# Four first products before the first second product, and a PSUM bank moved from transposes to first products

## The chip, the cores and the metric

The kernel runs on one core of a Trainium2 chip. The metric is device time in microseconds (us) of one execution. The kernel before takes 1392.38 us, the median of 3 runs (1392.05, 1392.38 and 1400.18 us).

## The reference

Three layers follow each other. An attention with queries averaged in pairs gives 2304 tokens of 512 numbers. A mixture of 8 experts sends each token to the one expert with the largest gate logit. A third layer works on all tokens with a cosine gate. All arrays that come in are 32-bit here except that the last layer's weights are narrowed by the kernel from 64-bit words.

```
xe = x[mask]                       # the tokens of expert e
h  = np.maximum(xe @ w1[e], 0.0)   # 512 -> 1024, the "first product"
ye = h @ w2[e]                     # 1024 -> 512, the "second product"
out[mask] = gate_w[mask, None] * ye
...
h = x @ w_in
g = h * np.cos(h)
return g @ w_out
```

## The kernel before

**Stages.** The attention of 4 batches by 8 heads comes first, with the routing of each batch's tokens after it. Then come the experts, in 12 units: a unit is up to 256 tokens of one expert. The units per expert are (3, 2, 2, 1, 1, 1, 1, 1), so units 0 to 2 belong to the busiest expert, and units 10 and 11 hold 128 tokens at most. The cosine layer in 5 blocks of up to 512 tokens ends the kernel.

**A unit.** Its tokens are gathered from memory and transposed on the PE into a PSUM tile of the pool `px` (tag `pt`), which ACT copies out as `xh` (line 1069) and DVE as the remainder `xl` (line 1070). The hidden width of 1024 is cut in four chunks. For a chunk, `first` (lines 903 to 926) makes 24 matmuls into one bank of the pool `ph`; ACT then writes `hh` with a relu (line 924), and DVE the remainder `hl` (line 925), so the bank is free when both are done. `second` (lines 951 to 966) makes 12 matmuls from `hh` and `hl` into the two banks of `py`. A chunk's `first` and `second` are called F0 to F3 and S0 to S3 below. The pending list holds `ahead` chunks, HP in number, before the oldest one's `second` is written; with HP = 2 the order is F0 F1 F2 S0 F3 S1 S2 S3. A unit's results go out with ACT (line 985) and DVE (line 986) and a DMA on ACT's queue (line 987). In units of 128 tokens (`tokens_first`, `turned`) the pending length is 0 whatever HP is, but their products and transposes also take `ph` tiles.

**Work between.** After S0, S1, S2 and S3 the function `second` writes the work of `between[c]`: in an expert's last unit the load of chunk c of the weights of the expert two further on, and two steps of `Narrow` in units 2 to 8. A load is two DMAs on SP's queue into three raw buffers, two casts on ACT (line 1057) and two subtractions on DVE or POOL (line 1058). A chunk's w2 cast overwrites the weights which the S of that chunk reads, two experts alternating between two sets. A step narrows a tile of 64-bit words: a DMA on SP's queue, four instructions on DVE (lines 1110, 1113, 1116, 1119), two on ACT (1115, 1118), two on POOL (1120, 1121), and a store on ACT's queue (1130), with four buffers of each kind. Steps are placed behind the latest relu on ACT's queue by `issue_after(self.relu)`.

**Order.** The program's order is a priority: a planner simulates the engines at build time and fixes each engine's queue, so instructions of different parts interleave (the transposes of a unit's tokens stand at the end of the unit before). On the chip each engine runs its queue in that order and waits at the head. The eight PSUM banks of this stage take the place of those of the attention, whose pools `at_ps2` (3), `at_psm` (3, also used by the routing) and `at_ps1` (2) are opened in this order.

Of the kernel before, what the change touches and what calls it, by code (L numbers as in the profile page):

```python
# [16 lines left out]
PSUM = bass.MemoryType.PSUM  # L17
# [27 lines left out]
class Attention:  # L45
# [15 lines left out]
    def __init__(self, tc, ctx, pools, q, k, v, ident, xpool):  # L61
        nc = self.nc = tc.nc
        self.tc = tc
        self.q, self.k, self.v = q, k, v
        self.ident = ident
        self.xpool = xpool

        cp, self.pw, self.pk, self.p3, ce, self.p1 = (pools[k] for k in "cwksep")
        self.ps2 = ctx.enter_context(tc.tile_pool(name="at_ps2", bufs=3, space=PSUM))
        self.psm = ctx.enter_context(tc.tile_pool(name="at_psm", bufs=3, space=PSUM))  # L70
        self.ps1 = ctx.enter_context(tc.tile_pool(name="at_ps1", bufs=2, space=PSUM))
        self.idr = cp.tile([P, P], F32R, name="idr")
        nc.vector.tensor_copy(self.idr, ident)
        self.k2, self.q1, self.q2, self.va, self.mm, self.qr, self.pe = [], [], [], [], [], [], []

        def const(kept, pools, name, shape, dt=F32):
            kept += [p.tile([P] + shape, dt, name=f"{name}_{i}") for i, p in enumerate(pools)]

        self.mx = []
        const(self.qr, (cp,) * 2, "qr", [5, 2 * D])  # L80
        const(self.mm, (cp,) * 2, "mm", [5, 3])
        const(self.pe, (cp,) * 2, "pe", [5, 66])
        const(self.mx, (cp,) * 4, "mx", [5], F32R)
        const(self.q1, (ce, ce, ce, cp), "q1", [SQ + 64], F32R)
        const(self.k2, (ce, cp, ce), "k2", [S], F32R)
        const(self.q2, (ce, ce, ce, cp), "q2", [SQ], F32R)
        const(self.va, (cp, cp, ce, ce, ce), "va", [NK, 130], F16)
        self.st = {}
        self.xf, self.xs = {}, {}
# [380 lines left out]
ZAT = 2  # L470
ZU = 11
MPOOL = ((), (0, 1, 2, 3))
HP = 2
NSTEP = (0, 2, 8, 8, 8, 8, 8, 8, 8, 6, 0, 0)

LOAD1 = ((1, 2), (1, 3), (2, 0), (2, 1))
# [406 lines left out]
class Experts:  # L883
    def __init__(self, tc, ctx, w1, w2, y_d, rp, ident, ahead):
        self.ahead = ahead
        self.tc, self.nc = tc, tc.nc
        self.w1, self.w2, self.y_d = w1, w2, y_d
        self.rp, self.ident = rp, ident
        self.p2 = ctx.enter_context(tc.tile_pool(name="ex_p2", bufs=2, reuse_waits="tile"))
        self.ph = ctx.enter_context(tc.tile_pool(name="ex_ph", bufs=3, space=PSUM, reuse_waits="tile"))  # L890
        self.px = ctx.enter_context(tc.tile_pool(name="ex_px", bufs=3, space=PSUM, reuse_waits="tile"))
        self.py = ctx.enter_context(tc.tile_pool(name="ex_py", bufs=2, space=PSUM, reuse_waits="tile"))

    def chunk(self, name, e, c, to):
# [312 lines left out]
def body(ctx, tc, q, k, v, w_gate, w1, w2, w_in, w_out, out):  # L1207
# [104 lines left out]
    with mid as s:  # L1312
        ns = ExitStack()
        nw = ns.enter_context(tc.tile_pool(name="nw", bufs=4, side="right", reuse_waits="tile"))
        ex = Experts(tc, s, w1, w2, y_d, rp, ident, HP)
        narrow = Narrow(nc, nw, jobs)
# [119 lines left out]
```

## Time and profile before

| | |
|---|---|
| median of 3 runs | 1392.38 us |
| the profiled execution's own time | 1388.87 us |
| its span on the core | 1387.3 us |
| mean granted clock of the PE | 0.955 |
| PE busy | 1246.8 us (90%) |
| DVE busy | 1081.0 us (78%) |
| ACT busy | 737.7 us (53%) |
| POOL busy | 674.3 us (49%) |

The busy times are sums over the whole span; the stages differ in what limits them, so the sections below read them by stretch. The profiled execution is 3.5 us under the median of the runs.

### The profile page before, as it was taken

The numbers are of one execution on the slowest core, as the hardware profiler recorded it, in microseconds if no ns is written. First come the engines' busy times: TensorE is split into PE (matmuls) and PEld (weight loads), VectorE is DVE, ScalarE is ACT, GpSimd is POOL, SyncE is SP. The second block draws the span as 40 slices with busy tenths as digits, with TensorE's granted clock in tenths as the row PEclk, the third lists the DMA queues.
The fourth block names the chain that finished last, engine by engine and source line by source line (L and its number), as shares of the span: only waits on it lengthen the run. The fifth ranks groups of instructions, "written<-read, shape, count | busy, mean of one in ns | idle before, by whom it ended". The sixth has DMA issues, their size and how long they took to land. (4 is left out here: it accounts for less than half of the span.)

```text
span 1387.3 us, 27417 instructions
## 1 busy us (share of the span) xinstructions
PE 1246.8 (90%) x10190; PEld 1051.3 (76%) x10190; DVE 1081.0 (78%) x2075; ACT 737.7 (53%) x1695; POOL 674.3 (49%) x623
## 2 busy tenths in 40 slices
PE   5897997999979998999799887889899999999996
PEld 4686886887768887878777776777687888888885
DVE  6996988888879998864598789896965666667674
ACT  4685875777758875872364455555322323222232
POOL 6684876666568777641367667675302002001010
PEclk9898999999989998999999898999999999999998
DMA  8348345333543342415687667787102001000000
GB/s 178 93 115 184 87 104 70 87 79 83 126 70 87 79 108 58 113 32 102 184 262 227 208 212 261 244 269 228 45 0 64 1 0 61 1 11 35 1 31 16
DMA packets 126911, 146.24 MB, mean 105 GB/s; under 512 B 35888, under 2 KB 83120, under 8 KB 126768
## 3 DMA queue, kind: packets, MB, share of 16 engines
q1 hardware_dynamic: 108784, 114.97, 32.7%
q0 software_dynamic: 5600, 15.25, 3.6%
q10 hardware_dynamic: 12384, 14.17, 3.4%
q8 instruction: 82, 1.34, 0.4%
q14 instruction: 61, 0.50, 0.1%
HBM read 97.57 MB, written 28.43 MB: 91 GB/s over the span
## 5 line engine op out<-in xcount | busy, mean ns | idle before, releaser
L319 POOL TENSOR_TENSOR pl<-pf,ph 128x576 f16<-128x576 f32 x220 | 310.5, 1420 | 138.3 <-ACT ph L309 59.3
L297 ACT ACTIVATE pf<-pst 128x288 f32<-128x288 f32 x576 | 222.0, 419 | 101.2 <-PE pst L289 84.2
L263 DVE TENSOR_REDUCE mm<-pm 128x1 f32<-128x384 f32 x432 | 226.7, 546 | 45.0 <-PE pm L254 37.5
L288 PE MATMUL pst<-q,k 128*128 128x288 f32 x576 | 195.6, 346 | 0.1
L289 PE MATMUL pst<-q,k 66*128 66x288 f32 x576 | 172.3, 308 | 24.5 <-DMA q<-mx 24.5
L484 POOL DMA_INDIRECT out_dram<-os,token x18 | 18.2, 1012 | 347.8 <-ACT os L1200 182.5
L338 PE MATMUL po<-va,pl 128*128 128x66 f16 (+1 forms) x1440 | 178.0, 197 | 1.9 <-DVE pl L319 1.0
L336 PE MATMUL po<-va,ph 128*128 128x66 f16 (+1 forms) x1440 | 179.4, 197 | 0.3 <-ACT pe L342 0.3
L337 PE MATMUL po<-va,ph 128*128 128x64 f16 (+1 forms) x1440 | 177.2, 196 | 0.0
L254 PE MATMUL pm<-k,q 128*128 128x384 f32 x384 | 151.2, 412 | 19.1 <-DVE mm L263 15.8
L1171 ACT ACTIVATE a<-a,hpi 128x512 f32<-128x512 f32 (+1 forms) x80 | 54.5, 681 | 210.8 <-DVE a L1170 210.8
L336 PEld LDWEIGHTS <-ph 128*128 128x128 f16 (+1 forms) x1440 | 136.4, 102 | 25.4 <-issue 11.2
L338 PEld LDWEIGHTS <-pl 128*128 128x128 f16 (+1 forms) x1440 | 137.8, 102 | 14.9 <-issue 5.6
L337 PEld LDWEIGHTS <-ph 128*128 128x128 f16 (+1 forms) x1440 | 138.0, 102 | 7.7 <-issue 2.5
L289 PEld LDWEIGHTS pst<-q,k 66*128 66x128 f32 x576 | 113.4, 198 | 26.5 <-DMA q<-mx 17.5
L309 ACT CAST ph<-pf 128x576 f16<-128x576 f32 x191 | 129.5, 681 | 1.4 <-PE po L337 0.4
L1161 PE MATMUL ch<-zh,w1h_m 128*128 128x512 f32 (+1 forms) x320 | 118.9, 372 | 4.5 <-ACTq L1385 3.4
L1161 PE MATMUL ch<-zl,w1h_m 128*128 128x512 f32 (+1 forms) x320 | 118.7, 371 | 0.0
L1161 PE MATMUL ch<-zh,w1l_m 128*128 128x512 f32 (+1 forms) x320 | 118.5, 370 | 0.0
L288 PEld LDWEIGHTS pst<-q,k 128*128 128x128 f32 x576 | 113.0, 197 | 4.9 <-ACT pf L297 1.3
L1185 PE MATMUL po<-w2h_m,gh 128*128 128x512 f32 x288 | 114.1, 396 | 0.0
L1185 PE MATMUL po<-w2l_m,gh 128*128 128x512 f32 x288 | 113.8, 395 | 0.0
(262 smaller groups left out, 3386.5 us busy)
## 6 DMA issues: line engine op xcount, KB each, us to landing
w1r_e<-in_moe_w_dram SPq DMA_DIRECT2D x32, 512.0 KB, 5.2
w2r_e<-in_moe_w_dram SPq DMA_DIRECT2D x32, 512.0 KB, 5.4
kr<-in_k_dram SPq DMA_DIRECT2D x32, 288.0 KB, 3.2
vr<-in_v_dram SPq DMA_DIRECT2D x32, 288.0 KB, 3.0
k<-k SPq DMA_DIRECT2D x32, 288.0 KB, 4.4
q<-q SPq DMA_DIRECT2D x60, 144.0 KB, 2.4
qr<-in_q_dram SPq DMA_DIRECT2D x32, 256.0 KB, 3.5
raw<-in_moe_w_in_dram SPq DMA_DIRECT2D x32, 256.0 KB, 4.2
```

The source lines that it names most:

```text
L254: nc.tensor.matmul(ps[:, :384], self.st[i]["q1"][:, q0 : q0 + P], self.st[i]["k1"][:, ks], start=True, stop=True)
L263: self.nc.vector.tensor_reduce(self.mm[i % 2][:, ci, g : g + 1], self.st[i]["pm", ci, g][:, :384], axis=AX.X, op=ALU.max)
L288: nc.tensor.matmul(ps[:, :288], s["k1"][:, ks], s["q1"][:, o], start=True, stop=False)
L289: nc.tensor.matmul(ps[:, :288], self.k2[i % 3][: D + 2, ks], self.q2[i % 4][: D + 2, o], start=False, stop=True)
L297: nc.scalar.activation(s["pf", c][:, j * 288 : (j + 1) * 288], s["pst", c, j][:, :288], AF.Exp, scale=0.0625)
L309: nc.scalar.copy(ph, pf)
L319: low = eng.tensor_sub(s["pl"][:, c, :], s["pf", c], s["ph"][:, c, :])
L336: nc.tensor.matmul(po[:, :66], hi, va[:, c, D:130], start=(c == 0), stop=False)
L337: nc.tensor.matmul(po[:, :D], hi, va[:, c, :D], start=False, stop=False)
L338: self.product = nc.tensor.matmul(po[:, :66], lo, va[:, c, D:130], start=False, stop=(c == NK - 1))
L1161: nc.tensor.matmul(ph[:, :n], wt[:, c, fs], z[:, c, :n], start=(k == 0), stop=(k == 3 * NDC - 1))
L1185: nc.tensor.matmul(po[j], g[:, ts], wt[:, f % FC, :], start=(f == 0 and k == 0), stop=(f == NFC2 - 1 and k == 2))
```

## The change

HP goes from 2 to 3, so that a unit's order becomes F0 F1 F2 F3 S0 S1 S2 S3, and the `hh` and `hl` tiles get four buffers in place of three. The pool `ph` gets four PSUM banks in place of three, and `px` two in place of three.

```diff
-HP = 2
+HP = 3
...
-        self.ph = ctx.enter_context(tc.tile_pool(name="ex_ph", bufs=3, space=PSUM, reuse_waits="tile"))
-        self.px = ctx.enter_context(tc.tile_pool(name="ex_px", bufs=3, space=PSUM, reuse_waits="tile"))
+        self.ph = ctx.enter_context(tc.tile_pool(name="ex_ph", bufs=4, space=PSUM, reuse_waits="tile"))
+        self.px = ctx.enter_context(tc.tile_pool(name="ex_px", bufs=2, space=PSUM, reuse_waits="tile"))
```

## Rows read from the trace of the kernel before

**Rows 1.** Busy time by stretch: PE, PEld, DVE, ACT, POOL; clock, DMA share, GB/s.
```profile
708.00:920.00 212.00, 179.22 (x1062) 155.75 (x1061) 186.81 (x318) 111.58 (x207) 148.24 (x140) 0.91 0.76 239
...
955.00:1387.30 432.30, 410.30 (x1883) 335.65 (x1881) 290.00 (x495) 125.67 (x202) 55.03 (x54) 0.99 0.09 29
```

**Rows 2.** The PE's timeline in units 3 to 9, its waits and one F3.
```profile
718.90 0.50 PE L957 MATMUL py_u<-w2h_e,hh_u 128*128 128x512 f32 x1 [2.03 <-ACT hh_u L924]
720.78 0.80 PE L957 MATMUL py_u<-w2h_e,hl_u 128*128 128x512 f32 x1 [1.14 <-DVE hl_u L925]
...
760.54 0.79 PE L957 MATMUL py_u<-w2h_e,hh_u 128*128 128x512 f32 x1 [2.24 <-ACT hh_u L924]
...
777.64 0.79 PE L957 MATMUL py_u<-w2h_e,hh_u 128*128 128x512 f32 x1 [3.07 <-ACT hh_u L924]
...
781.46 0.80 PE L957 MATMUL py_u<-w2h_e,hl_u 128*128 128x512 f32 x1 [2.60 <-DVE hl_u L925]
...
785.21 0.29 PE L918 MATMUL ph_u<-xh_e,w1h_e 128*128 128x256 f32 x1
...
788.06 0.39 PE L957 MATMUL py_u<-w2h_e,hh_u 128*128 128x512 f32 x1
...
807.60 0.50 PE L957 MATMUL py_u<-w2h_e,hh_u 128*128 128x512 f32 x1 [1.49 <-ACT hh_u L924]
810.60 0.50 PE L957 MATMUL py_u<-w2h_e,hl_u 128*128 128x512 f32 x1 [2.26 <-DVE hl_u L925]
...
839.22 0.79 PE L957 MATMUL py_u<-w2h_e,hh_u 128*128 128x512 f32 x1 [3.12 <-ACT hh_u L924]
846.25 0.80 PE L957 MATMUL py_u<-w2h_e,hl_u 128*128 128x512 f32 x1 [5.82 <-DVE ys_u L986]
...
874.08 0.33 PE L1067 MATMUL pt_e<-ident,xg_e 128*128 128x128 f32 x1 [2.13 <-DMA xg_e<-x_d,ix_e]
...
879.07 1.22 PE L957 MATMUL py_u<-w2h_e,hl_u 128*128 128x512 f32 x2 [4.67 <-DVE hl_u L925]
...
905.43 0.50 PE L957 MATMUL py_u<-w2h_e,hl_u 128*128 128x512 f32 x1 [1.73 <-DVE hl_u L925]
```

**Rows 3.** Busy time by stretch: units 4, 5 and 7, each from F0 to F0.
```profile
738.30:765.80 27.50, 25.26 (x156) 22.32 (x154) 21.81 (x43) 15.32 (x31) 18.65 (x19) 0.94 0.75 232
765.80:797.30 31.50, 25.83 (x155) 22.33 (x153) 25.78 (x48) 13.18 (x27) 19.63 (x21) 0.89 0.64 203
...
827.30:862.10 34.80, 25.86 (x156) 22.43 (x154) 33.86 (x55) 19.48 (x34) 27.05 (x23) 0.85 0.77 255
```

**Rows 4.** Busy time by stretch: S0 of unit 4, and S0 of unit 5.
```profile
746.90:749.70 2.80, 2.80 (x14) 2.29 (x13) 2.80 (x1) 1.56 (x4) 2.36 (x4) 1.00 0.48 171
777.60:785.20 7.60, 4.96 (x12) 3.52 (x13) 4.82 (x7) 2.27 (x5) 3.81 (x4) 0.55 0.70 245
```

**Rows 5.** DVE's waits, 687 to 920 us: total us, times, longest.
```profile
DVE v L1110 <- DMA wo_d<-v: 8.6, 5, 2.8
DVE w1l_e L1058 <- ACT w1h_e L1057: 4.6, 3, 2.4
...
DVE xl_e L1070 <- ACT xh_e L1069: 1.4, 1, 1.4
```

**Rows 6.** ACT's waits in the same stretch.
```profile
ACT w1h_e L1057 <- DMA w1r_e<-in_moe_w_dram: 27.8, 12, 6.2
...
ACT w2h_e L1057 <- PE py_u L957: 12.1, 2, 7.3
```

**Rows 7.** PE's timeline: F3 of unit 0, tokens of unit 2, unit 10.
```profile
637.27 0.28 PE L918 MATMUL ph_u<-xh_u,w1h_e 128*128 128x256 f32 x1
...
674.87 0.87 PE L1067 MATMUL pt_e<-ident,xg_e 128*128 128x128 f32 x4 [4.69 <-DMA xg_e<-x_d,ix_e]
...
926.60 0.44 PE L946 MATMUL phT_u<-ident,hs_u 128*128 128x128 f32 x2 [3.38 <-ACT hs_u L940]
```

**Rows 8.** DVE's timeline: it reads the last PSUM tile of the routing.
```profile
645.63 0.20 DVE L692 TENSOR_TENSOR ro<-pr,bo 128x40 f32<-128x40 f32 x1 [3.07 <-PE pr L682]
```

## The prediction

> **What bounds the kernel now.** I read the busy times by stretch first, since the change touches the expert stage alone. From 708 to 920 us, units 3 to 9, PE is busy for 179.2 of 212 us and DVE for 186.8, its densest stretch with all other queues working too; from 955 us to the end PE is busy for 410.3 of 432.3 us [rows 1]. So a microsecond that the expert stage hands over early is kept by the PE-bound cosine layer, and the question is what sets the pace in the 212 us.
>
> PE's timeline shows where it stands still: at the start of S0, waiting for `hh` of chunk 0 and then for `hl` of it [rows 2]. The waits are 2.03 + 1.14 = 3.17 us in unit 3, none in unit 4 (there S3 waits for 2.24), 3.07 + 2.60 = 5.67 in unit 5, 3.75 in unit 6, 8.94 in unit 7, 2.13 + 4.67 = 6.80 in unit 8 and 1.73 in unit 9, 32.3 us in all with unit 4's. F3 stands behind S0 in PE's queue. With three `ph` banks it could not have been started there anyway: its bank is chunk 0's, which the same late `hl` frees. PE is therefore held by a reader on another engine and by a missing bank together, which is what the change takes up.
>
> Then the side that makes `hl` late. DVE's and ACT's own waits name memory and each other more than PE: DVE waits 8.6 us for the buffer of a narrowing store, ACT 27.8 us for w1 to arrive, and for PE only 12.1 us, twice [rows 5, 6]. In unit 7, 34.8 us long, DVE is busy for 33.86 us [rows 3]: no reordering on PE makes that unit's side work shorter by more than a microsecond.
>
> **Part 1, F3 ahead of S0.** F3 takes 788.06 - 785.21 = 2.85 us [rows 2]. Put into the wait it hides min(2.85, wait): 2.85 in units 3, 5, 6, 7 and 8, 1.73 in unit 9, 15.98 us. The relu of chunk 3 now stands ahead of the load and steps of `between[0]` on ACT, so unit 4's 2.24 for `hh` at S3 should go as well: 18.2 us, the upper end, if `hl` of chunk 0 stays as late behind F0 as it is. The lower end is one 2.85: if DVE and ACT keep their absolute times, F3 gains its place once, and after that PE merely arrives 2.85 earlier at each S0 and waits 2.85 longer.
>
> Between these ends I look at what two neighbouring units did. S0 of unit 4 found its operands ready, and the unit took 27.5 us; unit 5 then waited for 5.67 and took 31.5, together 59.0 [rows 2, 3]. Time that PE won was largely given back one unit later, so I start from the lower end. What the side can speed up by is DVE's waiting for ACT, 4.6 + 1.4 = 6.0 us [rows 5], since ACT's relus no longer sit behind a weight cast that waits for S0. Of that I take half, 3.0; its ends are 0 and 6.0. Sum for units 3 to 9: 2.85 + 3.0 = 5.85.
>
> What is late next is `hl` of chunks 1 and 2, which S1 and S2 now want with no F3 between; S1 starts 2.80 us after S0, the length of an undisturbed S0 [rows 4]. That is part of why I don't take the upper end.
>
> **The wait also costs clock.** S0 of unit 5 has PE 4.96 us busy at a granted 0.55, near the lower of its two levels (1.2 and 2.4 GHz), against 2.80 at 1.00 in unit 4 [rows 4]. 2.16 us would come back there if the wait fell away; but 5.67 - 2.85 = 2.82 us of it stays, so I count none.
>
> **Part 2, what else moves.** Chunk 0's load and its two steps now follow the relu of chunk 3. On SP's and POOL's queues their order against other DMAs and gathers does not depend on a relu. On ACT they come later by at most F3's 2.85, hidden as long as S0 itself waits, since the w2 cast must wait for S0 in either order. Without that cover the cost is the slow rival below.
>
> Units 0 and 1 lie ahead of the stretch: PE waits 4.69 us there for the gathered tokens of unit 2 [rows 7], which come from the routing, so what PE wins before is waited for again. Zero. The fourth `ph` bank is one of the routing's: its last tile is read at 645.63 [rows 8], while unit 0's F3 starts at 637.27 [rows 7]. Bound: 8.4 us later, of which 4.69 are covered, so 0 to 3.7; I take 0, as the bank may be any of three and the planner can put S0 first.
>
> Two `px` banks hold the two transposed tiles of one unit, and the next unit's come over 25 us later [rows 3]. Zero, by that cover; without it a transpose would wait for DVE as S0 does now, 1.73 to 8.94 us. In units 10 and 11 PE waits 3.38 us for `hs` [rows 7]; a fourth `ph` bank lets a further product fill it: 0 to 3.4, I take 1.5.
>
> **Sum.** 5.85 + 1.5 = 7.35 us. Against the profiled execution (span 1387.3, itself 1388.87) that gives 1381.5; that execution is 3.5 us under the median of 1392.38. The median after is predicted at 1392.4 - 7.4 = 1385.0, with 1379 to 1391 as this case's own range (gains of 13 to 1).
>
> **Two rules that pull opposite ways.** The gaps ahead of S0 recur in six of seven units, with lengths from 1.73 to 8.94 [rows 2]. The Trainium skill ("Perfetto Trace Analysis", Optimization Strategy) says that a gap that repeats on the engine which should be saturated can mean there is not enough PSUM for the next tile. By it the fourth bank gives the upper end, 18.2 us; that the lengths differ fivefold speaks for a backlog instead. The same page (Identifying the Most-Contended Engine) judges Vector by occupancy and Tensor by the share of weight loads, and works on the highest first. Here that is DVE, 186.8 against 155.75 of 212 us [rows 1], and by it PE's order gives next to nothing.
>
> **Rivals.**
> - *Full gain, 0.21.* The side follows PE: relus and casts come earlier as S1 to S3 close up, each unit keeps its F3. 1392.4 - 18.2 = 1374. For it: DVE has 25 us without work in the 212 [rows 1], enough for 18. Against it: 8.6 of DVE's waits are for stores [rows 5].
> - *The side alone sets the pace, 0.23.* Only one F3 is won, or the planner goes on placing S0 ahead of F3 where it thinks `hl` is ready, and the change does not do what it says. 1389 to 1393. For it: unit 7 in rows 3, and the pair of units 4 and 5.
> - *Slower, 0.11.* Place: ACT's cast of w2 chunk 0, which waits for the end of S0. From the point where `hl` of chunk 0 is ready before F3 ends, S0 ends 2.85 later than now, and ACT's queue (steps, stores, the next relus) stands behind that cast. Units 4, 6, 7, 8 and 9 load weights: 5 x 2.85 = 14.3, so 1407. For it: this wait is 12.1 us already [rows 6]. Against it: only unit 4 has `hl` in time now.
> - The forecast has the remaining 0.45.
>
> **Range and chances.** About 1% (13.9 us) is what a measurement of this kernel can tell from no change. The range 1372 to 1396 holds the forecast, the full gain and the one-off, with the start's bound above it, and leaves out the slow case and some tails. Faster by over 1% (below 1378.5): nearly all of the full gain and a tail of the forecast, 0.21. Slower by over 1%: most of the slow case, 0.09. Within: 0.70.
>
> **What would show it.** In the trace after, PE's S matmuls of a unit should follow each other with F3 ahead of all. Right: waits at S0 shorter by under 3 us in unit 3, but not in the later units, whose S0 start a few us earlier in absolute time; DVE over 90% busy from 708 us. Full gain: those waits shorter by 2.85 each and the cosine layer starting some 18 us before 955. Slow: ACT's waits for `py_u` well above 12.1 us, and no wait of PE for `hl`. The prediction is wrong if the planner shuffles the steps and loads so that DVE's queue has another order altogether, which no row here can tell.

## The result: 1.3% slower

The changed kernel takes 1411.9 us, the median of four runs (1409.6 to 1416.33), against 1392.85 us for the kernel before in the same comparison (1392.05 to 1400.18). The ratio is 1.013, with a 95% interval of 1.0103 to 1.0157. That is 19 us more, outside the range of 1372 to 1396, and on the other side of the forecast. The profiled execution after takes 1411.51 us, its span is 1409.9 us and the mean granted clock 0.947.

The first reading is by stage. I cut both traces at PE's own marks: the attention's last product, the first product of unit 2, of unit 10 and of the cosine layer. These are the stretches before (columns: stretch in us and its length, then busy us and instruction count of PE, PEld (its weight loads), DVE, ACT and POOL; granted clock, DMA share, GB/s):

```profile
623.90:684.30 60.40, 53.30 (x329) 45.80 (x325) 31.88 (x114) 18.47 (x30) 15.54 (x16) 0.94 0.61 128
684.30:919.70 235.40, 202.62 (x1215) 176.85 (x1213) 203.84 (x345) 126.13 (x232) 159.50 (x150) 0.92 0.76 240
919.70:955.30 35.60, 30.14 (x178) 26.07 (x177) 28.68 (x39) 21.93 (x39) 20.41 (x18) 0.90 0.75 241
```

And the same stretches after, with units 3 to 9 alone as the third row and the cosine layer as the last:

```profile
628.50:699.10 70.60, 55.87 (x333) 48.21 (x332) 34.33 (x116) 18.95 (x30) 15.95 (x16) 0.82 0.48 118
699.10:928.70 229.60, 200.63 (x1212) 175.32 (x1210) 181.62 (x320) 121.78 (x225) 159.59 (x143) 0.92 0.75 233
722.50:928.70 206.20, 177.23 (x1059) 154.19 (x1057) 170.08 (x296) 108.01 (x200) 150.88 (x136) 0.91 0.76 236
928.70:979.70 51.00, 30.53 (x179) 26.04 (x176) 32.44 (x60) 30.16 (x52) 33.38 (x30) 0.84 0.84 267
979.70:1409.90 430.20, 411.78 (x1880) 337.38 (x1880) 283.75 (x495) 121.51 (x197) 46.81 (x49) 0.98 0.07 23
```

The spans differ by 22.6 us. The attention ended 4.6 us later (628.5 against 623.9), which is no effect of the change: up to there PE, DVE, ACT and POOL run the same instructions in the same order, and the attention's end lies between 622.0 and 635.1 us over all the traces of this study. The start of the experts costs 10.2 (60.4 to 70.6). Units 2 to 9 gain 5.8 (235.4 to 229.6), and units 10 and 11 lose 15.4 (35.6 to 51.0). The cosine layer is 1.8 shorter (1387.3 - 955.3 = 432.0, and 430.2). So in this trace the middle of the stage, which the prediction worked out most closely, came near what it said (the experiments below show that the nearness is within the scatter), and two edges that it had priced at nothing, or as a small gain, decided the time.

**The start.** PE's timeline after, just behind the attention (start, duration, instruction; in brackets the idle time before it and what ended it):

```profile
642.17 0.19 PE L675 MATMUL pr<-oh,tri 128*128 128x40 f16 x1 [6.20 <-DVE oh L654]
642.20 0.26 PE L677 MATMUL pr<-oh,ones 128*128 128x32 f16 x4
642.31 0.28 PE L682 MATMUL pr<-oh,ones 128*128 128x8 f16 x5
642.44 0.56 PE L918 MATMUL ph_u<-xh_u,w1h_e 128*128 128x256 f32 x1
...
672.26 1.09 PE L1067 MATMUL pt_e<-ident,xg_e 128*128 128x128 f32 x4 [5.30 <-DMA xg_e<-x_d,ix_e]
```

The first product of unit 0 stands directly behind the last products of the routing, at 642.44, that is 13.9 us after the attention's end. Before, it came 0.1 us after that end, and F3 of unit 0 started at 637.27 while the routing still ran [rows 7]. PE's wait for the tokens of unit 2 is still there, 5.30 us against 4.69 [rows 7]. The 10.2 us of this stretch are 7.6 more without work on PE (70.60 - 55.87 = 14.7 against 60.40 - 53.30 = 7.1) and 2.6 more busy, at a granted clock of 0.82 in place of 0.94. The 13.9 us ahead of F0 are not all lost, as PE makes the routing's products in them, which before ran between those of unit 0.

**Units 3 to 9.** The same view, the waits ahead of second products that answer to those of before [rows 2], of a microsecond or more:

```profile
759.98 0.50 PE L957 MATMUL py_u<-w2h_e,hh_u 128*128 128x512 f32 x1 [1.27 <-ACT hh_u L924]
765.15 0.80 PE L957 MATMUL py_u<-w2h_e,hl_u 128*128 128x512 f32 x1 [4.43 <-DVE hl_u L925]
...
794.45 0.79 PE L957 MATMUL py_u<-w2h_e,hl_u 128*128 128x512 f32 x1 [3.42 <-DVE hl_u L925]
...
852.84 0.79 PE L957 MATMUL py_u<-w2h_e,hh_u 128*128 128x512 f32 x1 [7.22 <-ACT hh_u L924]
859.71 0.80 PE L957 MATMUL py_u<-w2h_e,hl_u 128*128 128x512 f32 x1 [5.65 <-DVE hl_u L925]
...
887.55 0.50 PE L957 MATMUL py_u<-w2h_e,hl_u 128*128 128x512 f32 x1 [1.77 <-DVE hl_u L925]
...
915.15 0.51 PE L957 MATMUL py_u<-w2h_e,hh_u 128*128 128x512 f32 x1 [3.36 <-ACT hh_u L924]
```

Unit 3's waits are down from 3.17 us to 0.74, unit 7's are up from 8.94 to 12.87. All waits of PE in these units add up to 29.0 us, 32.8 before.

**Units 10 and 11.** PE's timeline again:

```profile
939.32 0.69 PE L946 MATMUL phT_u<-ident,hs_u 128*128 128x128 f32 x2 [7.08 <-ACT hs_u L940]
...
976.49 1.97 PE L1067 MATMUL pt_y<-ident,yg 128*128 128x128 f32 x8 [10.49 <-DVE zl L1070]
```

The wait for `hs` has doubled (3.38 before [rows 7]), and there is a new one: the transposes `pt_y`, which prepare the cosine layer's tokens, wait 10.49 us until DVE has read an earlier `pt` tile into `zl`. That looks like the price of the missing `px` bank. The fourth experiment shows that it isn't.

**What ACT waits for.** Over units 2 to 11 after (waiting line, what it waited for: total us, times, longest):

```profile
ACT t L1115 <- POOL l L1120: 25.3, 18, 6.6
ACT w1h_e L1057 <- DMA w1r_e<-in_moe_w_dram: 22.7, 13, 4.9
ACT l L1118 <- POOL v L1121: 17.4, 14, 3.2
ACT hh_u L924 <- POOL v L1121: 12.5, 2, 7.1
```

and before, over the same units:

```profile
ACT w1h_e L1057 <- DMA w1r_e<-in_moe_w_dram: 28.4, 13, 6.2
ACT l L1118 <- POOL v L1121: 16.8, 14, 6.5
ACT w2h_e L1057 <- PE py_u L957: 12.1, 2, 7.3
...
ACT t L1115 <- POOL l L1120: 8.2, 9, 1.7
```

The cast of w2 waiting for PE is gone from the first places. In its stead ACT waits three times as long for one tile of the narrowing steps: `t` at line 1115 needs a free buffer of four, and the reader that frees it is POOL's product `l` at line 1120.

### The profile page after: what moved, and what is told of

Its sections match the earlier page's. It is cut to its first block, busy times and chain, and to the rows that moved or that the text cites. A ratio compares the mean times of both kernels' runs of the same rounds, so it can differ in the third digit from the quotient of the medians.

```text
span 1409.9 us, 27413 instructions
## 1 busy us (share of the span) xinstructions
PE 1246.6 (88%) x10190; PEld 1051.8 (75%) x10190; DVE 1061.5 (75%) x2075; ACT 738.0 (52%) x1695; POOL 680.6 (48%) x623
## 3 DMA queue, kind: packets, MB, share of 16 engines
q1 hardware_dynamic: 108784, 114.97, 32.8%
```

## The experiments

The table gives, for every trace, the us from the attention's end to unit 2's first product, of units 2 to 9, of units 10 and 11, and the sum of the last two (unit 2 to the cosine layer); then the median and the ratio to the kernel before in the same comparison, with its interval. The kernel before took 1392.85 us in the first comparison and 1397.6 to 1401.52 in the later ones, so medians of different comparisons are set side by side by their ratios alone.

| kernel | to unit 2 | 2 to 9 | 10, 11 | unit 2 to cosine | median us | ratio |
|---|---|---|---|---|---|---|
| before | 60.5 | 235.4 | 35.7 | 271.1 | 1392.85 | |
| before_again | 62.3 | 235.2 | 33.9 | 269.0 | 1397.42 | 0.9977 [0.9941, 1.0013] |
| after | 70.6 | 229.6 | 51.0 | 280.6 | 1411.9 | 1.013 [1.0103, 1.0157] |
| banks_only | 76.1 | 238.7 | 36.4 | 275.1 | 1409.92 | 1.0073 [1.0044, 1.0103] |
| order_only | 60.6 | 243.8 | 42.1 | 285.9 | 1405.63 | 1.0039 [1.0012, 1.0065] |
| swap_pools | 68.3 | 236.0 | 50.0 | 286.1 | 1408.09 | 1.0057 [1.0025, 1.0088] |
| y_in_ph | 72.4 | 236.0 | 53.4 | 289.4 | 1421.02 | 1.0148 [1.0094, 1.0201] |
| thin_before | 61.8 | 198.3 | 39.4 | 237.7 | 1361.88 | 0.9703 [0.9659, 0.9747] |
| thin_after | 70.6 | 193.7 | 34.8 | 228.5 | 1362.68 | 0.9732 [0.97, 0.9764] |
| steps_back | 72.6 | 237.2 | 42.8 | 280.0 | 1415.15 | 1.0104 [1.0069, 1.0139] |
| own_fourth | 63.5 | 231.6 | 50.9 | 282.5 | 1408.54 | 1.0061 [1.0036, 1.0086] |
| own_fourth_hp2 | 65.3 | 233.9 | 40.7 | 274.6 | 1402.66 | 1.0008 [0.9982, 1.0033] |
| own_fourth_spread | 64.0 | 242.9 | 38.4 | 281.3 | 1410.09 | 1.0101 [1.0026, 1.0177] |
| own_fourth_buffers | 65.8 | 230.0 | 40.4 | 270.4 | 1398.49 | 0.9998 [0.9967, 1.0028] |
| changed_buffers | 71.6 | 229.3 | 41.0 | 270.3 | 1405.28 | 1.0051 [1.0034, 1.0068] |
| before_buffers | 62.1 | 229.9 | 43.0 | 272.8 | 1393.64 | 0.9964 [0.9939, 0.999] |
| before_all_buffers | 68.5 | 234.1 | 41.6 | 275.8 | 1407.21 | 1.0067 [1.0036, 1.0098] |

The stage columns are of one profiled execution each; before and before_again, the same kernel, differ by 1.8, 0.2, 1.8 and 2.1 in them. That is too fine a measure: after, swap_pools and y_in_ph have the same instructions in the same order on PE, DVE, ACT and POOL in units 3 to 9, and these units take 206.2, 212.7 and 212.5 us (here swap_pools, then y_in_ph).

```profile
724.00:936.70 212.70, 178.24 (x1059) 155.50 (x1058) 174.37 (x299) 110.24 (x202) 151.02 (x136) 0.90 0.74 233
727.60:940.10 212.50, 175.75 (x1059) 153.28 (x1058) 172.03 (x300) 109.70 (x203) 150.19 (x136) 0.91 0.75 234
```

So a difference of 6 us in a column may be the execution's alone. The two traces of the kernel before are also of executions of 1388.87 and 1395.69 us, below its medians in the later comparisons: there the columns of the other kernels add up to 3 to 10 us more over the kernel before than the medians do, and in swap_pools, whose traced execution took 1419.24 us against a median of 1408.09, to 15. The columns show where time went; how much a change costs is read from the ratios.

**banks_only** keeps the new banks and takes the old order; **order_only** the reverse.

```diff
 # banks_only, on the changed kernel
-HP = 3
+HP = 2
 # order_only, on the kernel before
-HP = 2
+HP = 3
```

> Four ph banks and two px banks with HP = 2 (order F0 F1 F2 S0 F3 as before). Theory (the loss is the bank move: at the start the first products of unit 0 stand behind the whole routing because their pool now takes a bank of the routing's, about +10 us net; at the end the third transpose of the cosine layer's tokens waits for one of two px banks, +5 to +15): 1408 to 1418 us, unit 0's F0 some 14 us later than before relative to the attention's end. Rival (the loss is the order F0 to F3 itself, through a later hl and the backlog on DVE): 1390 to 1396 us.

> HP = 3 with the banks of before (three ph, three px). Theory: F3 now stands ahead of S0 in PE's queue and waits for chunk 0's bank, that is for the same hl that S0 waited for; nothing is won or lost at start and end: 1389 to 1396 us. Rival (the order itself costs): 1405 us or more.

Both halves are slower, by 0.73% and 0.39%, and together they come near the 1.3% of the change. The order alone was expected to cost nothing. The halves have different places. With the banks alone, PE's timeline begins the experts as late as after the whole change:

```profile
640.82 0.19 PE L675 MATMUL pr<-oh,tri 128*128 128x40 f16 x1 [7.17 <-DVE oh L654]
640.84 0.25 PE L677 MATMUL pr<-oh,ones 128*128 128x32 f16 x4
640.95 0.27 PE L682 MATMUL pr<-oh,ones 128*128 128x8 f16 x5
641.09 0.56 PE L918 MATMUL ph_u<-xh_u,w1h_e 128*128 128x256 f32 x1
```

14.8 us after the attention's end; with the order alone it is 0.1 us after it. The order alone loses behind unit 2's start: 285.9 us to the cosine layer in place of 271.1.

**swap_pools** opens the attention's PSUM pools in another order, so that other banks lie under the fourth `ph` bank.

```diff
-        self.psm = ctx.enter_context(tc.tile_pool(name="at_psm", bufs=3, space=PSUM))
         ...
+        self.psm = ctx.enter_context(tc.tile_pool(name="at_psm", bufs=3, space=PSUM))
```

> The changed kernel with the attention's PSUM pools opened in the order ps2, ps1, psm, so that the four ph banks take no bank of the routing's pool (py and one px bank do). Theory: unit 0's first products run again beside the routing, F0 right at the attention's end; 1396 to 1404 us, with the loss at the end left as it is (PE's wait for zl near 10 us). Rival (order itself): 1409 us or more.

Unit 0 now starts 0.1 us after the attention, but the stretch to unit 2 is still 68.3 us, because PE stands in front of the tokens of unit 2 instead:

```profile
PE pt_e L1067 <- DMA xg_e<-x_d,ix_e: 15.8, 1, 15.8
```

So which bank it is decides where unit 0 starts; by itself this layout did not give back the time that was expected of it (1.0057). This experiment left the start open, and own_fourth took it up again.

**y_in_ph** gives the cosine layer's first transposes a `ph` bank, so that they no longer wait for one of the two `px` banks.

```diff
-                    nc, zp[0], xq, "xg", ex.px, "pt", ident, ...
+                    nc, zp[0], xq, "xg", ex.ph, "ph", ident, ...
```

> The changed kernel with the cosine layer's first token transposes put into ph banks instead of px banks. Theory: PE's wait of 10.5 us for zl at the end goes, the start keeps its loss: 1398 to 1406 us. Rival (order itself, or the wait only moves to the next one): 1409 us or more.

The wait moved with the bank and kept its size, 10.8 us in place of 10.49:

```profile
PE ph_u L935 <- DVE zl L1070: 10.8, 1, 10.8
PE pt_y L1067 <- DMA yg<-y_d,source: 6.0, 2, 4.8
```

Units 10 and 11 take 53.4 us. The bank is where the wait shows, not its cause: `zl` itself is late, on DVE. In the trace after, `zl` waits for `zh`, and `zh` stands on ACT's queue behind a cast of the cosine layer's weights that waits for its load:

```profile
974.12 1.04 ACT L1057 CAST w2h_m<-w2r_m 128x1024 fp32r<-128x1024 f32 x1 [3.14 <-DMA w2r_m<-wo_d]
975.07 1.07 ACT L1069 CAST zh<-pt_y 128x512 fp32r<-128x512 f32 x2
975.74 1.29 DVE L1070 TENSOR_TENSOR zl<-pt_y,zh 128x512 fp32r<-128x512 f32 x2 [5.73 <-ACT zh L1069]
```

The load reads `wo_d`, which the narrowing steps fill.

**thin_before** and **thin_after** leave out most of each narrowing step, so that the side work is light: of a step's eight compute instructions only the first is left. The cosine layer then works with weights that are not the narrowed ones.

```diff
         nc.vector.tensor_scalar(v, hi, 3, 0x3FFFFFFF, ...)
-        ... (seven further instructions on DVE, ACT and POOL)
         self.store()
```

> The kernel before with the narrowing steps thinned: of a step's 8 compute instructions only the first DVE one is left (its DMA in and its store stay; the last layer's weights are then not the narrowed ones). Base for the next run. Theory (DVE, ACT, POOL and the narrowing chain set the pace of units 2 to 11): 20 us or more less than the kernel before. Rival (PE's own order sets it): less than 10 us less.

> The changed kernel with the same thinning (the last layer's weights are not the narrowed ones). Theory (the loss behind unit 10 is the narrowing chain, pushed back behind the relu of F3 and delivered at the end): with the chain light that loss is gone and only the start's 10 us stay, 0 to +12 us against the thinned kernel before, and PE's wait for zl under 3 us. Rival (the loss at the end is the two px banks or PE's order itself): +17 us or more, and the wait for zl stays near 10 us.

Units 2 to 9 and 10 to 11 of the light kernels, before and then after:

```profile
696.90:895.20 198.30, 190.38 (x1218) 168.62 (x1216) 97.86 (x176) 83.92 (x112) 51.21 (x35) 1.00 0.90 287
895.20:934.60 39.40, 29.91 (x179) 26.06 (x178) 20.01 (x27) 24.31 (x40) 13.75 (x10) 0.88 0.74 240
```

```profile
698.50:892.20 193.70, 190.33 (x1212) 170.04 (x1210) 92.79 (x171) 82.65 (x110) 48.50 (x34) 0.98 0.90 285
892.20:927.00 34.80, 29.68 (x179) 25.89 (x177) 20.78 (x27) 22.05 (x38) 11.32 (x9) 0.90 0.81 246
```

Without the narrowing the change is worth 237.7 - 228.5 = 9.2 us behind unit 2's start in these two traces, and the 15 us at the end are gone. The start's loss remains (61.8 against 70.6) and eats it: the two medians are 0.8 us apart. So the loss at the end needs the narrowing steps.

**steps_back** asks whether their place does it: chunk 0's two steps, which the change puts behind F3, go back between F2 and F3.

```diff
             pend.append((c, first(c)))
+            if c == self.ahead - 1:
+                ...          # the two steps of between[0], left out behind S0
```

> The changed kernel with the two narrowing steps of between[0] written between F2 and F3 as before (queued behind the relu of chunk 2), PE's order F0 to F3 and the banks as in the change. Theory (steps squeezed behind F3's relu are late): 5 to 13 us less than the changed kernel, that is +6 to +14 us against the kernel before, the last step no more than 5 us later behind the start of unit 2 than before (256 us). Rival (the place of the steps does not matter): +16 us or more, last step near 268 us behind the start of unit 2.

It only shifts the loss, 237.2 + 42.8 = 280.0 in place of 229.6 + 51.0 = 280.6, though the last instruction of the last step now starts 260 us behind unit 2's first product, in place of 268. The place of these two steps isn't the cause.

**own_fourth** puts the fourth `ph` bank into a pool of its own, used by F3 alone. **own_fourth_hp2** is the same with the old order.

```diff
-        self.ph = ctx.enter_context(tc.tile_pool(name="ex_ph", bufs=4, ...))
+        self.ph = ctx.enter_context(tc.tile_pool(name="ex_ph", bufs=3, ...))
+        self.ph3 = ctx.enter_context(tc.tile_pool(name="ex_ph3", bufs=1, ...))
...
-            ph = self.ph.tile([P, FC, U], F32, tag="ph", name=f"ph_{name}_{c}")
+            ph = (self.ph3 if c == 3 else self.ph).tile([P, FC, U], F32, tag="ph", ...)
```

> The changed kernel with the fourth ph bank in a pool of its own (first products of chunk 3 only), so the pool of F0 to F2 takes no bank of the routing's. Theory (the start's loss is the pool as a whole waiting for the routing): F0 of unit 0 right at the attention's end, and unit 2 some 60 us behind it in place of 70; +7 to +11 us against the kernel before, as the loss at the end stays. Rival (the start's loss is the order F0 to F3): unit 2 at 68 us or later, +16 us or more.

> The banks of own_fourth (F3 in a bank of its own, two px banks) with HP = 2, so the order F0 F1 F2 S0 F3 of before. Theory (behind unit 2 it is the order F0 to F3 that delays the work between): 268 to 276 us from unit 2 to the cosine layer, 0 to +4 us in all against the kernel before. Rival (the banks cost behind unit 2 as well): 279 us or more, +6 us or more.

Here PE goes from the attention straight into unit 0, F0 in line 919 (one line lower than after, as one line was added):

```profile
633.18 0.19 PE L338 MATMUL po<-va,pl 128*64 128x66 f16 x1
633.31 0.39 PE L919 MATMUL ph_u<-xh_u,w1h_e 128*128 128x256 f32 x1
```

The same banks, the same count, and 0.1 us in place of 13.9: in the one pool of four, F0 too was queued behind the routing's last products, though only one of the pool's banks had been the routing's. Unit 2 starts at 63.5 us, so 7 of the 10 us are back. What is not back shows as a longer wait for the tokens of unit 2, 12.0 us where before had 4.69:

```profile
687.60 1.11 PE L1068 MATMUL pt_e<-ident,xg_e 128*128 128x128 f32 x4 [12.01 <-DMA xg_e<-x_d,ix_e]
```

The ratio falls from 1.013 to 1.0061, which leaves the loss behind unit 2 (282.5). The variant with the old order can't be told from the kernel before by its runs (1.0008): a fourth bank with two `px` banks brings nothing and costs nothing clear of the scatter.

**own_fourth_spread** adds an even placing to own_fourth: one narrowing step behind each F and each S, not two behind each S. This was to test whether two steps at a time overrun the chain's buffers.

```diff
             pend.append((c, first(c)))
+            beside(c, 0)     # the first half of between[c]'s steps
...
-            for k, g in (between or {}).get(c, ()):
+            beside(c, 1)     # the loads and the other half
```

> own_fourth with one narrowing step behind each of F0 to F3 and one behind each of S0 to S3, in place of two behind each S. Theory A (the burst): 6 to 10 us less than own_fourth, unit 2 to cosine 272 to 277 us in place of 282.5, so about the time of the kernel before. Theory B (the place of the steps only moves the loss between the units and the end): within 3 us of own_fourth.

The even placing does not take the loss away: 242.9 + 38.4 = 281.3, and 1.0101, where about the time of the kernel before was expected.

**own_fourth_buffers** gives the tiles `v64` and `t64` of a narrowing step five buffers, not four; **before_again** runs the kernel before beside it. Then **changed_buffers** does the same to the changed kernel, **before_buffers** to the kernel before, and **before_all_buffers** gives the old order a fifth buffer for every tile of that pool.

```diff
-        v = p.tile(shape, I32, name="v64")
-        t = p.tile(shape, I32, name="t64")
+        v = p.tile(shape, I32, name="v64", bufs=5)
+        t = p.tile(shape, I32, name="t64", bufs=5)
 # before_all_buffers
-        nw = ns.enter_context(tc.tile_pool(name="nw", bufs=4, ...))
+        nw = ns.enter_context(tc.tile_pool(name="nw", bufs=5, ...))
```

> own_fourth with five instead of four buffers for the tiles v64 and t64 of the narrowing steps. Theory A (the eight steps of a unit come in one burst behind F3's relu, and the chain stalls on its four buffers): 4 to 9 us less than own_fourth, ACT's wait of L1115 for POOL well under 19 us. Theory B (the order of the planned queues, not the buffers): within 3 us of own_fourth.

> The kernel before once more, for a second trace of it: how far the stages of one program differ from trace to trace. The time from F0 of unit 2 to the first cosine product was 271.1 us and from the attention's end to F0 of unit 2 60.5; if they come back within 3 us, differences of 9 us between kernels in these stretches are the kernels' own. If they scatter by 8 us or more, the stage sums of single traces say little.

> The changed kernel as it is, with five v64 and t64 buffers. Theory (two losses that add: the pool's wait at the start, about 10 us, and the chain's buffers, about 9): the second goes and the first stays, +7 to +12 us against the kernel before, unit 2 to cosine 268 to 273 us, F0 of unit 0 still 14 us behind the attention. Rival (the gain of own_fourth_buffers came from another placing of the queues, not from the buffers): +16 us or more.

> The kernel before with five v64 and t64 buffers. Theory (only with F0 to F3 first does the narrowing chain run into its four buffers; with S0 between, other waits set the pace): within 4 us of the kernel before, unit 2 to cosine 266 to 272 us. Rival (the buffers help any order by the same 9 us, so the order F0 to F3 still costs what it did): 7 us or more less than the kernel before, unit 2 to cosine 262 us or less.

> The kernel before with five buffers for all four narrowing tiles (raw, v, t, l). Theory (the chain is not what bounds this order): within 4 us of the kernel before. Rival (it is): 6 us or more less; this would be the version that beats both kernels.

With the new order a fifth buffer is worth 10.3 us behind unit 2's start (280.6 to 270.3), and 12.1 on top of own_fourth (282.5 to 270.4). With the old order it is worth nothing there (271.1 and 269.0 without, 272.8 with). The ratios agree: 1.013 to 1.0051 with the start's loss left in (71.6 us), and 1.0061 to 0.9998 without it. Over all traces with the narrowing whole, the new order takes 280.0 to 289.4 us there with four buffers (seven kernels) and 270.3 and 270.4 with five; the old order takes 269.0 to 275.8. ACT's waits over units 2 to 11 of changed_buffers, the first and the one in question:

```profile
ACT w1h_e L1057 <- DMA w1r_e<-in_moe_w_dram: 32.9, 13, 8.2
...
ACT t L1115 <- POOL l L1120: 6.2, 3, 4.4
```

25.3 us became 6.2. The last instruction of the last narrowing step starts 241 us after unit 2's first product, where after the change it was 268 and before it 256.

What the fifth buffer did on the way is less certain than its worth. The planner knows the number of buffers too and laid other queues: of DVE's 496 instructions between the attention's end and the cosine layer, at most 348 stand in the same order in after and changed_buffers. Whether the time came from the free buffer on the chip or from the queues that the planner made of it, no run separates. That a number of buffers can cost time is seen in before_all_buffers: it was expected within 4 us of the kernel before and is 0.67% slower, with unit 2 reached at 68.5 us; why is not shown.

Both losses taken away together, own_fourth_buffers equals the kernel before and doesn't beat it. Its units 2 to 9 take 230.0 us, but units 10 and 11 take 40.4: seven subtractions of expert weights (line 1058 of the kernel before) are still to be done when unit 10 starts, four in the kernel before. Before_buffers, with the old order and the old banks, has the lowest ratio of the kernels that do the whole work, 0.36% under the kernel before; but before_again, the same program as before, came out 0.23% under it, so this gain is not shown.

## Why the prediction was wrong

**The bound, right.** What the expert stage hands over is kept: the cosine layer takes 428.7 to 433.9 us in all 17 traces. The stage's length is what counts.

**Units 3 to 9, near in one trace, and in part by luck.** Forecast 5.85 us, found 211.6 - 206.2 = 5.4. But swap_pools and y_in_ph, with the same queues there, take 212.7 and 212.5, which is no gain over the 211.6 and 211.3 of the two traces of before. That F3 gains its place about once, and PE then waits at a later S, is seen in the waits: 0.74 in place of 3.17 in unit 3, 29.0 in place of 32.8 in all. Two of the waits that I took for late `hh` and `hl` were others by their own rows [rows 2]: the 5.82 in unit 7 is put down to DVE's copy `ys`, and the 2.13 in unit 8 is for gathered tokens. The clock, counted at nothing, is 0.91 in these units before and after. But the sign that I named, DVE over 90% busy, isn't there. DVE is busy for 170.08 of 206.2 us, 82%, and was for 88% before. And the sign of being wrong that I named last, another order on DVE's queue, is there: of its 496 instructions between the attention's end and the cosine layer, at most 338 stand in the order of before.

**First step that failed: the fourth `ph` bank at nothing.** I had the price "0 to 3.7" and took 0, "as the bank may be any of three and the planner can put S0 first". The bound was already wrong: it let F3 alone wait for the routing, and counted the wait for unit 2's tokens as cover. The runs show that the first product of the whole pool is put behind the routing (F0 after the attention's end: banks_only 14.8 us, order_only 0.1, own_fourth 0.1), and that PE's wait for the tokens was not shortened by it (5.30 us). Price: 10 us.

**Second step that failed: the moved load and steps on ACT, "hidden as long as S0 itself waits".** I looked at when ACT's casts come and not at how the chain of narrowing steps is buffered. One step is eight instructions, on DVE, DVE, ACT, DVE, ACT, DVE, POOL and POOL, with four `v` and four `t` buffers, on the same queues as `hh` and `hl`. In unit 7 after, each engine's timeline shows the next waiting for the last. DVE waits for a store to free a `v` buffer, POOL for DVE's `t`, ACT for POOL's `l`, and `hh` of the unit, which PE wants, stands behind that on ACT:

```profile
839.29 0.30 DVE L1110 TENSOR_SCALAR v<-raw 128x256 int32<-128x256 int32 x1 [4.68 <-DMA wi_d<-v]
...
843.55 3.71 POOL L1120 TENSOR_TENSOR l<-l,t 128x256 f32<-128x256 f32 x2 [6.25 <-DVE t L1119]
...
846.43 0.43 ACT L1115 ACTIVATE t<-raw 128x256 f32<-128x256 f32 x1 [6.61 <-POOL l L1120]
...
852.18 0.61 ACT L924 ACTIVATE hh_u<-ph_u 128x512 fp32r<-128x512 f32 x1
```

PE's S0 starts on that `hh` at 852.84, after its wait of 7.22 us. The unit takes 39.7 us, against 34.8 before. The other traces bear that out: 40.1 and 40.7 us in y_in_ph and swap_pools, 35.7 in before_again, 34.3 and 34.0 in the two kernels with the new order and five buffers. Priced by ratios, this step and the next together cost 0.6 to 0.8%, which the fifth buffer takes back.

**Third: units 10 and 11, "0 to 3.4, I take 1.5", came out at 15.4 the other way.** I priced the bank there, and not the work that arrives late. The steps that are behind end in these units. When unit 10 starts, eight steps have their last instruction still to come, against five and four in the two traces of before. POOL is busy for 33.38 us there in place of 20.41, `zh` stands behind the cast of weights that came late (974.12 above), and PE waits 10.49. What held that cast's load, the late steps or its own buffers, is not shown. This isn't the `px` pool, whose change I priced at zero: own_fourth_hp2 has two `px` banks at 1.0008, and y_in_ph shows the same wait on a `ph` bank.

**The rivals.** The slow rival named 1407, near the 1411.9 found, but its place is not where the time went. ACT's wait of the w2 cast for PE, 12.1 us before, should have grown, and it is no longer among ACT's longer waits. Of the full gain thin_after shows 9 us, not 18, behind unit 2's start, once the side work is light. "The side alone sets the pace" was nearest to the mechanism, but it saw the side as work, and the side was waiting.

**The two rules.** The Trainium skill ("Perfetto Trace Analysis", Optimization Strategy) says that a repeating gap on the engine that should be saturated can mean too little SBUF or PSUM for the next tile, and names the number of buffers. The prediction took up PSUM alone, and no run here bears that out: a fourth bank with the old order gives 1.0008. For SBUF the runs agree once the order is F0 to F3: a fifth buffer of the tiles `v` and `t` takes 1.013 to 1.0051. The same page of the Trainium skill (Identifying the Most-Contended Engine) would have put DVE first. That the side work bounds these units is borne out by thin_before: DVE's busy time in units 2 to 9 falls from 203.84 to 97.86 us, and the units from 235.4 to 198.3. The loss by the change is not seen in that measure: DVE's idle time between unit 2 and the cosine layer grew from 38.5 us (271.0 - 232.5) to 66.5 (280.6 - 214.1) while the stretch grew by 9.6.

**What stays open.** Why the new order runs into the four buffers is not shown: steps_back and own_fourth_spread, which place the steps differently, halve the wait of `t` for POOL, to 12.7 and 14.0 us, and gain no time. That a fifth buffer takes the loss away under the new order is shown twice, that it does nothing of that size under the old one once; the path between is read from unit 7 alone. The variants with an own fourth bank reach unit 2 one to five us later than the kernel before, as its tokens come later (PE first turns them 54.4 to 56.1 us after the attention's end, 51.1 and 51.9 before); why they do, the traces don't tell.

## To carry to other kernels

A PSUM bank that goes from one stage's pool to the next stage's can put the first tiles of the whole receiving pool behind the earlier stage, not just the one on that bank: look at what the bank did in the stage before, and if that is late, give it a pool of its own. When an order changes on the engine that is waiting, ask of each side chain on the other engines how many buffers it has and who stands behind it in the queue; here the chain that ran short of buffers cost 5 us in one unit, and most of its delay fell due at the stage's end. A wait for a bank names the reader that is late, so move the tile to another bank and see whether the wait moves along before the bank is blamed.

## What the runs showed that I had not expected

The attention, whose queues are the same in every kernel here, ended between 622.0 and 635.1 us, and that alone moves a span by up to 1%. Two single traces are therefore compared by stretches that begin and end at the same instructions, as in the table. Stretches with the same queues still differed by 6.5 us. And a lower busy time of DVE does not mean a shorter stage: between unit 2 and the cosine layer it was busy for 18 us less after the change, with nearly the same number of instructions (380 and 384), and the stretch was 9.6 us longer.
